# Folding three of eight q k products on VectorE before the head sums on TensorE, with q and k chunked by every second feature

## The chip, the cores and the metric

The kernel runs on one core of a Trainium2 chip. The metric is the device time of one execution in microseconds (us); of several runs the median is taken. Engines are called by their names in the profile: PE is TensorE's matmul, PEld its weight load, DVE is VectorE, ACT ScalarE, POOL GpSimd, SP the engine that issues most DMAs.

## What is computed

One input x of 2048 tokens by 512 features goes through a layer norm to xn. Two branches read xn and both are added to x.

```python
def _A_ref(x, wqkv, wo):             # H = 32 heads of Dh = 16
    W, dil = (8, 2)
    q, k, v = ...                    # from x @ wqkv
    off = jnp.arange(W) * dil        # each token sees itself and 7 tokens before it, in steps of 2
    logits = jnp.einsum('bhsd,bhswd->bhsw', q, kg) * scale
    attn = _softmax(where(mask, logits, -1e9))
    return einsum('bhsw,bhswd->bhsd', attn, vg) ... @ wo

def _B_ref(x, w_in, w_sp, b_sp, w_out):
    z = _gelu(x @ w_in)              # 2 x 688 features
    z1, z2 = z[..., :688], _layernorm(z[..., 688:])
    g = jnp.einsum('ts,bsf->btf', w_sp, z2) + b_sp
    return (z1 * g) @ w_out

out = x + _A_ref(xn, wqkv, wo) + _B_ref(xn, w_in, w_sp, b_sp, w_out)
```

## The kernel before

The order of instructions on every engine is the order in which the program writes them; nothing is reordered by a planner. Tiles wait for one another through semaphores, and a tile that lies over memory of a closed pool waits for the last use of what lay there. Tokens are handled in 16 tiles of 128. For attention they are split into two halves, hb = 0 and 1, of 1024 tokens, and each half into four groups of 256.

*Layer norm, transposes, z2.* In the first 30 us of the span the layer norm is made and xn is transposed into xnT (feature on the partition). z2_tile(i) (L235) makes one tile of gelu(xn @ w_in) for the second half of the features.

*q and k.* qk_pair (L289) and qk_chunk (L277) multiply 512 tokens with a chunk c of 128 columns of wqkv, 4 chunks for q and 4 for k, four accumulating matmuls of 512 columns each. ScalarE copies the result into qk[hb], with one feature per partition. Chunk c holds features 128c to 128c + 127, which is eight whole heads.

*Logits.* The eight distances are handled in pairs. products(hb, p) (L318) multiplies q with k at two distances, all four chunks, in one VectorE instruction of 8192 elements a partition. reduce_heads(hb, p) (L327) sums over the 16 features of a head, which lie on partitions: a 0/1 matrix rsel sends the 128 partitions of chunk c to its heads, and the four chunks accumulate in PSUM. The four token groups go to four 32-column tiles of the array, which run side by side. ScalarE copies the sums into lg (L329). softmax_top (L334 to L339), softmax_exp (L342, on ScalarE) and softmax_norm (L348 to L353) make the weights a_sb.

*Values.* v_pair (L302) makes v with a strided view of wv: every 16th column, for one feature of all 32 heads.

*The gated branch.* z2_norm (L269) normalises the 16 tiles of z2 on VectorE, one instruction each. mix(j) (L512) is the product of row block j of w_sp with all z2, 32 matmuls; ScalarE empties it into gs (L515), and the next row block j + 5 is loaded by a transposing DMA on SP. z1_tile(j) (L524) makes the matching tile of z1 with a gelu on ScalarE (L529), and gate_out(j) (L534) multiplies the two on VectorE; SP sends the product transposed into uT. There are three z1 tiles and four gs tiles.

mix and z1_tile take pairs of PSUM banks in turn. For tiles above 3 there are two pairs, so that mix(j + 1) takes the pair that mix(j) had, and z1_tile(j + 1) that of z1_tile(j).

*Between the stages.* From mix(0) on, TensorE goes through mix and z1_tile for j = 0 to 15. In the first three of these VectorE still ends the logits and the softmax; then from a queue of steps, av_ops, vector_work(us) takes steps until their written costs add up to the argument. A step is one product of v with the weights (L578, pw), an add (L583, L585, L587 into op), or softmax_norm for hb = 1. The order at this place is:

```python
g0 = mix(0)
products(1, 3)
z1_tile(0, g0)
g1 = mix(1)
softmax_norm(0, lgp)
z1_tile(1, g1)
gate_out(0)
g2 = mix(2)
reduce_heads(1, 2)
reduce_heads(1, 3)
softmax_top(1)
gate_out(1)
z1_tile(2, g2)
softmax_exp(1)
```

*The end.* out_b (L659) multiplies uT with w_out and out_a (L668) multiplies op with wo. For token groups jj = 0 and 1 out_b comes first, for jj = 2 and 3 out_a. op_rest carries two of the 16 features of op into free rows of uT, for hb = 0 by SP and for hb = 1 by ScalarE's queue. store adds x (the xr tiles) on VectorE (L675) and sends the result out; sums for jj = 2 take the banks that the stores of jj = 0 empty.

Of the kernel before, what the change touches and what calls it, by code (L numbers as in the profile page):

```python
# [7 lines left out]
BF16 = mybir.dt.bfloat16  # L8
F32 = mybir.dt.float32
ACT = mybir.ActivationFunctionType  # L10
ALU = mybir.AluOpType
PSUM = bass.MemoryType.PSUM

P = 128
# [3 lines left out]
C = D // P  # L18
# [11 lines left out]
TG = SB // NG  # L30
# [17 lines left out]
def kernel(  # L48
# [16 lines left out]
    V = nc.vector  # L65
    A = nc.scalar
    G = nc.gpsimd
    PE = nc.tensor
# [7 lines left out]
    const = ctx.enter_context(tc.tile_pool(name="const", bufs=1))  # L76
    base = ctx.enter_context(tc.tile_pool(name="base", bufs=1))
# [4 lines left out]
    pair_b = ExitStack()  # L82
# [4 lines left out]
    def bank_pair(name, two=False):  # L87
        turn[0] += 1
        pool = ps_b if turn[0] % 3 == 0 and not two else ps_a
        return pool.tile([P, 2, 512], F32, name=name, tag="mm")  # L90
# [9 lines left out]
    def spin(n):  # L100
        for _ in range(n):
# [5 lines left out]
    G.memset(ident[:], 0.0)  # L107
    G.affine_select(out=ident[:], in_=ident[:], compare_op=ALU.not_equal, fill=1.0,
                    base=0, pattern=[[-1, P]], channel_multiplier=1)
    rsel = const.tile([P, C, 32], BF16, name="rsel")  # L110
    G.memset(rsel[:], 1.0)
    for c in range(C):
        G.affine_select(out=rsel[:, c, :], in_=rsel[:, c, :], compare_op=ALU.is_ge, fill=0.0,
                        base=128 * c, pattern=[[-16, 32]], channel_multiplier=1)
        G.affine_select(out=rsel[:, c, :], in_=rsel[:, c, :], compare_op=ALU.is_ge, fill=0.0,
                        base=15 - 128 * c, pattern=[[16, 32]], channel_multiplier=-1)
    mask = const.tile([32, W, HALO], F32, name="mask")
    G.memset(mask[:], 0.0)
    G.affine_select(out=mask[:], in_=mask[:], compare_op=ALU.is_ge, fill=NEG,
                    base=-DIL * (W - 1), pattern=[[DIL, W], [1, HALO]], channel_multiplier=0)  # L120
# [22 lines left out]
    xnT = rpool.tile([P, C, S], BF16, name="xnT")  # L143
# [11 lines left out]
    wqk = e1.tile([P, C, 2, D], BF16, name="wqk")  # L155
# [95 lines left out]
    def z2_moments(i):  # L251
        for hh in range(2):
            V.bn_stats(zst[:, i, hh, :], z2[:, i, hh * FHALF:(hh + 1) * FHALF])
        V.bn_aggr(zmv[:, i, :], zst[:, i, :, :])
# [11 lines left out]
    def z2_norm():  # L266
        V.reciprocal(zrstd[:], zrstd[:])
        for i in range(NT):
            V.tensor_scalar(z2[:, i, :], z2[:, i, :], zmv[:, i, 0:1], zrstd[:, i:i + 1],  # L269
                            ALU.subtract, ALU.mult)  # L270

    def qk_chunk(b, c):
        tsl = slice(b * 512, (b + 1) * 512)
        pq = bank_pair("pq")
        for s in range(2):
            for kc in range(C):
                PE.matmul(pq[:, s, :], wqk[:, kc, s, c * P:(c + 1) * P], xnT[:, kc, tsl],  # L277
                          start=(kc == 0), stop=(kc == C - 1))
        at = HALO + b % 2 * 512
        A.copy(qk[b // 2][:, :, c, at:at + 512], pq[:])  # L280

    def qk_pair(b, s, c2):

        tsl = slice(b * 512, (b + 1) * 512)
        pq = bank_pair("pq")
        for cc in range(2):
            c = 2 * c2 + cc
            for kc in range(C):
                PE.matmul(pq[:, cc, :], wqk[:, kc, s, c * P:(c + 1) * P], xnT[:, kc, tsl],  # L289
                          start=(kc == 0), stop=(kc == C - 1))  # L290
        at = HALO + b % 2 * 512
        A.copy(qk[b // 2][:, s, 2 * c2:2 * c2 + 2, at:at + 512], pq[:])
# [15 lines left out]
    def shifted(ap):  # L308

        return bass.AP(ap.tensor, ap.offset, [ap.ap[0], [DIL, 2]] + list(ap.ap[1:]))  # L310

    lg = [lgp.tile([P, W, TG], BF16, name="lg") for _ in range(NB)]
    prs = {}

    def products(hb, p):
        pr = (prx if (4 * hb + p) % 3 == 2 else prp).tile([P, 2, C, SB], BF16, name="pr")
        off = HALO - DIL * (W - 1 - 2 * p)
        V.tensor_tensor(pr[:], qk[hb][:, 0, :, HALO:HALO + SB].unsqueeze(1).broadcast_to([P, 2, C, SB]),  # L318
                        shifted(qk[hb][:, 1, :, off:off + SB]), ALU.mult)
        prs[hb, p] = pr  # L320

    def reduce_heads(hb, p):
        pr = prs.pop((hb, p))
        pl = ps_aux.tile([P, 2, TG], F32, name="pl", tag="aux")
        for c in range(C):
            for k in range(NG):
                PE.matmul(pl[32 * k:32 * k + 32, :, :], rsel[:, c, :], pr[:, :, c, k * TG:(k + 1) * TG],  # L327
                          start=(c == 0), stop=(c == C - 1), tile_position=(0, 32 * k))
        A.activation(lg[hb][:, 2 * p:2 * p + 2, :], pl[:], ACT.Copy, scale=float(DH) ** -0.5)  # L329

    def softmax_top(hb):
# [9 lines left out]
    def softmax_exp(hb):  # L341
        A.activation(a_sb[:, :, hb * TG:(hb + 1) * TG], lg[hb][:], ACT.Exp)  # L342

    def softmax_norm(hb, pool):
        hsl = slice(hb * TG, (hb + 1) * TG)
        s4 = pool.tile([P, 4, TG], F32, name="s4", bufs=1)
        r1 = pool.tile([P, TG], BF16, name="r1", bufs=1)
        V.tensor_tensor(s4[:], a_sb[:, 0:4, hsl], a_sb[:, 4:8, hsl], ALU.add)  # L348
        V.tensor_tensor(s4[:, 0:2, :], s4[:, 0:2, :], s4[:, 2:4, :], ALU.add)
        V.tensor_tensor(s4[:, 0, :], s4[:, 0, :], s4[:, 1, :], ALU.add)  # L350
        V.reciprocal(s4[:, 0, :], s4[:, 0, :])
        V.tensor_copy(r1[:], s4[:, 0, :])
        V.tensor_tensor(a_sb[:, :, hsl], a_sb[:, :, hsl],  # L353
                        r1[:].unsqueeze(1).broadcast_to([P, W, TG]), ALU.mult)
# [3 lines left out]
    def load_wsp(j):  # L358
        t = wspp.tile([P, NT, P], BF16, name="wspT")
        SP.dma_start_transpose(t[:], B_w_sp[j * P:(j + 1) * P, :])  # L360
        wsps[j] = t
# [97 lines left out]
    reduce_heads(0, 1)  # L459
    reduce_heads(0, 2)  # L460
    products(0, 3)
    z2_moments(7)
    z2_moments(8)
    v_pair(0)
# [26 lines left out]
    v_pair(5)  # L491
    reduce_heads(1, 1)
    products(1, 2)
    softmax_exp(0)
    v_pair(6)
    v_pair(7)
# [11 lines left out]
    def mix(j):  # L508
        pg = bank_pair("pg", j > 3)
        for k in range(NT):  # L510
            for hh in range(2):
                PE.matmul(pg[:, hh, 0:FHALF], wsps[j][:, k, :], z2[:, k, hh * FHALF:(hh + 1) * FHALF],  # L512
                          start=(k == 0), stop=(k == NT - 1))
        gs = gsp.tile([P, 2, FHALF], BF16, name="gs")
        A.activation(gs[:], pg[:, :, 0:FHALF], ACT.Identity, bias=b_col[:, j:j + 1])  # L515
        if j + 5 < NT:
            load_wsp(j + 5)
        return gs

    def z1_tile(j, gs):  # L520
        pz = bank_pair("pz1", j > 3)
        for hh in range(2):
            for kc in range(C):
                PE.matmul(pz[:, hh, 0:FHALF], xnT[:, kc, j * P:(j + 1) * P],  # L524
                          w_z1[:, kc, hh * FHALF:(hh + 1) * FHALF],
                          start=(kc == 0), stop=(kc == C - 1))
        z1 = z1p.tile([P, FPAD], BF16, name="z1")
        G.memset(z1[:, FH:FPAD], 0.0)  # L528
        A.activation(z1[:, 0:FH].rearrange("p (a b) -> p a b", a=2), pz[:, :, 0:FHALF], ACT.Gelu_apprx_tanh)  # L529
        gate[j] = (gs, z1)  # L530

    def gate_out(j):
        gs, z1 = gate.pop(j)
        V.tensor_tensor(z1[:, 0:FH], gs[:].rearrange("p a b -> p (a b)"), z1[:, 0:FH], ALU.mult)  # L534
        SP.dma_start_transpose(uT[:, :, j * P:(j + 1) * P], z1[:])

    g0 = mix(0)
    products(1, 3)
    z1_tile(0, g0)
    g1 = mix(1)  # L540
    softmax_norm(0, lgp)
    z1_tile(1, g1)
    gate_out(0)
    g2 = mix(2)
    reduce_heads(1, 2)
    reduce_heads(1, 3)
    softmax_top(1)
    gate_out(1)
    z1_tile(2, g2)
    softmax_exp(1)  # L550
    att.close()

# [42 lines left out]
    def vector_work(us):  # L595
        while us > 0:
            t = next(work, None)
            if t is None:
                return
            us -= t  # L600
# [6 lines left out]
        SP.dma_start(xr[:], x_g[jj // 2, jj % 2])  # L607
        xrs.append(xr)

    vector_work(2.0)  # L610
    for j in range(3, NT):
        z1_tile(j, mix(j))
        if j == 3:
            pair_b.close()
            ps_o = [ctx.enter_context(tc.tile_pool(name="ps_o0", bufs=4, space=PSUM, reuse_waits="tile"))]
        vector_work(4.6)
        gate_out(j - 1)
        if j == 5:
            SP.dma_start(wout[:, 0:MCH - 1, :], B_w_out[0:(MCH - 1) * P, :].rearrange("(m p) n -> p m n", p=P))
            SP.dma_start(wout[0:FTAIL, MCH - 1, :], B_w_out[(MCH - 1) * P:FH, :])  # L620
            for e in range(2):
                SP.dma_start(wout[64 + 32 * e:96 + 32 * e, MCH - 1, :],
                             A_wo.rearrange("(h d) n -> d h n", d=DH)[DHA + e])
        if 6 <= j < 10:
            k = j - 6
            SP.dma_start(wo_r[32 * k:32 * k + 32, :, :], A_wo.rearrange("(h d) n -> h d n", d=DH)[:, 0:DHA, :])
        if 11 <= j < 13:
            load_xr(j - 11)
        if j == 13:
            op_rest(0, SP)  # L630
# [95 lines left out]
```

## Time and profile before

| what | value |
|---|---|
| median of 3 runs | 205.79 us (205.72 to 206.36) |
| profiled execution | 206.46 us |
| its span in the profile | 204.6 us |
| granted TensorE clock | 0.998 |
| matmuls | 1660 |
| q and k: L277 and L289 | 128 matmuls, 128x512 |
| head sums: L327 | 128 matmuls, 128x512, 32 columns of the array each |
| products: L318 | 8 of 4.42 us on VectorE |

The span is the time that the profile covers; the 1.9 us around it belong to the execution. A row of the groups gives the line of the program, the engine, the operation with its output and inputs and their shapes, how many there were, the busy time in us and the mean of one in ns, and the engine's idle time before them with what ended it. Busy times of one engine may overlap, above all those of matmuls, whose ends are modelled; the time that a series of matmuls takes is read from the chain or the timeline.

### The profile page before, as it was taken

The page shows a single profiled execution, that of the slowest core. Times are in us where ns is not written, and L with a number is a line of the kernel's source. Part 1 is how long each engine was busy: PE and PEld are TensorE (multiplying, and loading weights), DVE is VectorE, ACT ScalarE, POOL GpSimd, SP SyncE. Part 2 cuts the span into 40 slices and gives each one's busy share as a digit, 9 for nine tenths or more (in the row PEclk, how much of TensorE's full clock was granted, in tenths as well). Part 3 has the DMA queues.
Part 4 walks back from the last instruction along what each step waited for, and adds up shares of the span by engine and source line. Part 5 has one row for each costly group of instructions (what it writes and reads, how often), then busy time and mean ns, then how long its engine had stood idle before and what let it go on. Part 6 is the DMA issues. An engine that isn't in the chain of part 4 may idle for free.

```text
span 204.6 us, 4053 instructions
## 1 busy us (share of the span) xinstructions
PE 200.0 (98%) x1660; PEld 120.8 (59%) x1660; DVE 171.3 (84%) x210; ACT 89.4 (44%) x130; POOL 16.7 (8%) x82
## 2 busy tenths in 40 slices
PE   7899999999999999999999999999999999999994
PEld 7655554546666666656666666666666664444442
DVE  4799949979699999959999999999999988335163
ACT  4768986665889875335733321223333311000000
POOL 5035640000000100100000000000000000000000
PEclk9999999999999999999999999999999999999999
DMA  5984857996000006435957799999656224015633
GB/s 175 323 259 79 177 108 151 217 198 143 0 0 3 3 0 98 91 75 126 125 112 160 181 196 194 219 175 178 130 144 141 54 48 80 10 37 161 235 106 99
DMA packets 67410, 25.63 MB, mean 125 GB/s; under 512 B 57168, under 2 KB 67264, under 8 KB 67264
## 3 DMA queue, kind: packets, MB, share of 16 engines
q1 hardware_dynamic: 66976, 25.24, 56.7%
q8 instruction: 13, 0.21, 0.5%
q10 hardware_dynamic: 416, 0.14, 0.3%
q14 instruction: 5, 0.04, 0.1%
HBM read 9.79 MB, written 2.10 MB: 58 GB/s over the span
## 4 chain that ended last, share of the span: by engine, by line
PE 95%; DMA 3%; SPq 1%; DVE 0%; issue 0%
PE pg L512 37%; PE pq L277 10%; PE po L659 10%; PE pz L524 9%; PE pzb L235 9%; PE pv L302 7%; PE po L668 6%; PE pl L327 3%; PE pq L289 3%; DMA w_z<-in_B_w_in_dram 3%; PE po L641 1%; SPq L178 0%; PE pt L218 0%; SPq L176 0%; DVE ot L643 0%; SPq L175 0%
## 5 line engine op out<-in xcount | busy, mean ns | idle before, releaser
L512 PE MATMUL pg<-z,wspT 128*128 128x344 bf16 x512 | 77.3, 310 | 0.0
L512 PEld LDWEIGHTS <-wspT 128*128 128x128 bf16 x512 | 50.0, 98 | 24.9 <-issue 0.4
L318 DVE TENSOR_TENSOR pr<-qk 128x8192 bf16<-128x8192 bf16 x8 | 35.0, 4420 | 2.7 <-ACT qk L280 1.5
L515 ACT ACTIVATE gs<-pg,b_col 128x688 bf16<-128x688 f32 x16 | 13.3, 832 | 54.4 <-PE pg L512 54.4
L578 DVE TENSOR_TENSOR pw<-vp,a_sb 128x4096 bf16<-128x4096 bf16 x16 | 36.1, 2284 | 0.0
L277 PE MATMUL pq<-xnT,wqk 128*128 128x512 bf16 x96 | 21.4, 380 | 0.0
L524 PE MATMUL pz<-w_z,xnT 128*128 128x344 bf16 x128 | 21.3, 310 | 0.0
L235 PE MATMUL pzb<-w_z,xnT 128*128 128x344 bf16 x128 | 20.0, 310 | 0.5 <-DMA w_z<-in_B_w_in_dram 0.3
L659 PE MATMUL po<-wout,uT 128*128 128x512 bf16 x90 | 19.8, 380 | 0.0
L583 DVE TENSOR_TENSOR pw<-pw 128x4096 bf16<-128x4096 bf16 x8 | 18.3, 2288 | 0.1
L675 DVE TENSOR_TENSOR ot<-po,xr 128x512 bf16<-128x512 f32 x15 | 9.7, 686 | 9.3 <-PE po L668 6.9
L235 PEld LDWEIGHTS <-xnT 128*128 128x128 bf16 x128 | 12.3, 98 | 7.3 <-issue 0.5
L524 PEld LDWEIGHTS <-xnT 128*128 128x128 bf16 x128 | 12.4, 98 | 6.5 <-issue 0.4
L277 PEld LDWEIGHTS <-wqk 128*128 128x128 bf16 x96 | 9.3, 98 | 11.1 <-issue 0.4
L280 ACT CAST qk<-pq 128x1024 bf16<-128x1024 f32 x12 | 12.1, 1012 | 6.8 <-PE pq L277 6.8
L659 PEld LDWEIGHTS <-uT 128*128 128x128 bf16 x90 | 8.7, 98 | 10.7 <-issue 0.4
L302 PE MATMUL pv<-xnT,wv 128*32 128x512 bf16 x256 | 14.8, 380 | 0.0
L529 ACT ACTIVATE z<-pz 128x688 bf16<-128x688 f32 x16 | 11.9, 743 | 5.6 <-PE pz L524 5.2
L242 ACT ACTIVATE z<-pzb 128x688 bf16<-128x688 f32 x16 | 11.8, 739 | 2.2 <-PE pzb L235 2.2
L528 POOL MEMSET z<- 128x80 bf16 x16 | 3.1, 199 | 115.9 <-DMA uT<-z 61.2
L302 PEld LDWEIGHTS <-wv 128*32 128x32 bf16 x256 | 9.8, 140 | 4.2 <-issue 0.3
L668 PE MATMUL po<-wo_r,op 32*128 32x512 bf16 x224 | 12.3, 375 | 0.0
(85 smaller groups left out, 178.7 us busy)
## 6 DMA issues: line engine op xcount, KB each, us to landing
xr<-in_A_x_dram SPq DMA_DIRECT2D x4, 512.0 KB, 4.2
out_dram<-ot SPq DMA_DIRECT2D x15, 128.0 KB, 1.8
wo_r<-in_A_wo_dram SPq DMA_DIRECT2D x4, 448.0 KB, 4.9
xq<-in_A_x_dram SPq DMA_DIRECT2D x2, 512.0 KB, 7.8
wqk<-in_A_wqkv_dram SPq DMA_DIRECT2D x2, 512.0 KB, 7.8
w_z<-in_B_w_in_dram SPq DMA_DIRECT2D x2, 344.0 KB, 4.4
w_z<-in_B_w_in_dram SPq DMA_DIRECT2D x1, 688.0 KB, 5.7
wout<-in_B_w_out_dram SPq DMA_DIRECT2D x1, 640.0 KB, 4.6
```

The source lines that it names most:

```text
L235: PE.matmul(pz[:, hh, 0:FHALF], xnT[:, kc, i * P:(i + 1) * P], w_z2[:, kc, hh * FHALF:(hh + 1) * FHALF], start=(kc == 0), stop=(kc == C - 1))
L277: PE.matmul(pq[:, s, :], wqk[:, kc, s, c * P:(c + 1) * P], xnT[:, kc, tsl], start=(kc == 0), stop=(kc == C - 1))
L280: A.copy(qk[b // 2][:, :, c, at:at + 512], pq[:])
L302: PE.matmul(pv[32 * k:32 * k + 32, dd, :].rearrange("p (b t) -> p b t", b=NB), wv_v[:, kc, 2 * d2 + dd, :], xnT_g[:, kc, :, k, :], start=( ...
L318: V.tensor_tensor(pr[:], qk[hb][:, 0, :, HALO:HALO + SB].unsqueeze(1).broadcast_to([P, 2, C, SB]), shifted(qk[hb][:, 1, :, off:off + SB]), ...
L512: PE.matmul(pg[:, hh, 0:FHALF], wsps[j][:, k, :], z2[:, k, hh * FHALF:(hh + 1) * FHALF], start=(k == 0), stop=(k == NT - 1))
L515: A.activation(gs[:], pg[:, :, 0:FHALF], ACT.Identity, bias=b_col[:, j:j + 1])
L524: PE.matmul(pz[:, hh, 0:FHALF], xnT[:, kc, j * P:(j + 1) * P], w_z1[:, kc, hh * FHALF:(hh + 1) * FHALF], start=(kc == 0), stop=(kc == C - 1))
L578: V.tensor_tensor(pw[:], shifted(vp[:, :, hb, off:off + P]), a_sb[:, 2 * p:2 * p + 2, osl].unsqueeze(2).broadcast_to([P, 2, DH, P]), ALU.mult)
L583: V.tensor_tensor(pws[p - 1][:], pws[p - 1][:], pw[:], ALU.add)
L659: PE.matmul(pos[jj, k][:], uT[:, m, i * P:(i + 1) * P], wout[:, m, :], start=first and m == 0, stop=not first and m == MCH - 1)
L668: PE.matmul(pos[jj, k][:], op[32 * k:32 * k + 32, d, jj * P:(jj + 1) * P], wo_r[32 * k:32 * k + 32, d, :], start=first and d == 0, stop=(n ...
```

## The change

The features of q and k are put into chunks in another way. Chunk c now holds the features 256 (c mod 2) + 2j + (c div 2) for j = 0 to 127: every second feature of one half of the 512. Chunks c and c + 2 then hold, on the same partition, two neighbouring features of the same head. So one matrix rsel serves both, with 8 partitions to a head, and has two parts in place of four.

Because of that the two can be added before the sum over partitions. A new function fold does it on VectorE, in place, for three of the eight product tiles, (0, 3), (1, 2) and (1, 3); for these reduce_heads runs over two chunks instead of four. The weights of q and k are read with a step of two elements.

Around mix(0) to mix(3) the order is changed: gate_out(0) goes ahead of softmax_norm(0), gate_out(1) and z1_tile(2) ahead of reduce_heads(1, 2), and mix(3) and z1_tile(3) ahead of softmax_exp(1). The step of av_ops that came ahead of mix(3) is no longer taken there (vector_work(2.0) is gone), so that each later call takes steps that come one earlier in the queue than before.

```diff
-    rsel = const.tile([P, C, 32], BF16, name="rsel")
+    rsel = const.tile([P, 2, 32], BF16, name="rsel")
     G.memset(rsel[:], 1.0)
-    for c in range(C):
-        G.affine_select(out=rsel[:, c, :], in_=rsel[:, c, :], compare_op=ALU.is_ge, fill=0.0,
-                        base=128 * c, pattern=[[-16, 32]], channel_multiplier=1)
-        G.affine_select(out=rsel[:, c, :], in_=rsel[:, c, :], compare_op=ALU.is_ge, fill=0.0,
-                        base=15 - 128 * c, pattern=[[16, 32]], channel_multiplier=-1)
+    for g in range(2):
+        G.affine_select(out=rsel[:, g, :], in_=rsel[:, g, :], compare_op=ALU.is_ge, fill=0.0,
+                        base=128 * g, pattern=[[-8, 32]], channel_multiplier=1)
+        G.affine_select(out=rsel[:, g, :], in_=rsel[:, g, :], compare_op=ALU.is_ge, fill=0.0,
+                        base=7 - 128 * g, pattern=[[8, 32]], channel_multiplier=-1)
...
+    wqk_v = wqk[:].rearrange("p k s (g j e) -> p k s e g j", g=2, e=2)
+
     def qk_chunk(b, c):
...
-                PE.matmul(pq[:, s, :], wqk[:, kc, s, c * P:(c + 1) * P], xnT[:, kc, tsl],
+                PE.matmul(pq[:, s, :], wqk_v[:, kc, s, c // 2, c % 2], xnT[:, kc, tsl],
...
     def qk_pair(b, s, c2):
...
-                PE.matmul(pq[:, cc, :], wqk[:, kc, s, c * P:(c + 1) * P], xnT[:, kc, tsl],
+                PE.matmul(pq[:, cc, :], wqk_v[:, kc, s, c // 2, c % 2], xnT[:, kc, tsl],
...
+    def fold(hb, p):
+
+        pr = prs[hb, p]
+        V.tensor_tensor(pr[:, :, 0:2, :], pr[:, :, 0:2, :], pr[:, :, 2:4, :], ALU.add)
+        folded.add((hb, p))
+
+    folded = set()
+
     def reduce_heads(hb, p):
         pr = prs.pop((hb, p))
         pl = ps_aux.tile([P, 2, TG], F32, name="pl", tag="aux")
-        for c in range(C):
+        n = 2 if (hb, p) in folded else C
+        for c in range(n):
             for k in range(NG):
-                PE.matmul(pl[32 * k:32 * k + 32, :, :], rsel[:, c, :], pr[:, :, c, k * TG:(k + 1) * TG],
-                          start=(c == 0), stop=(c == C - 1), tile_position=(0, 32 * k))
+                PE.matmul(pl[32 * k:32 * k + 32, :, :], rsel[:, c % 2, :], pr[:, :, c, k * TG:(k + 1) * TG],
+                          start=(c == 0), stop=(c == n - 1), tile_position=(0, 32 * k))
...
     products(0, 3)
+    fold(0, 3)
     z2_moments(7)
...
     products(1, 2)
+    fold(1, 2)
     softmax_exp(0)
...
     g0 = mix(0)
     products(1, 3)
+    fold(1, 3)
     z1_tile(0, g0)
     g1 = mix(1)
+    gate_out(0)
     softmax_norm(0, lgp)
     z1_tile(1, g1)
-    gate_out(0)
     g2 = mix(2)
+    gate_out(1)
+    z1_tile(2, g2)
     reduce_heads(1, 2)
     reduce_heads(1, 3)
     softmax_top(1)
-    gate_out(1)
-    z1_tile(2, g2)
+    z1_tile(3, mix(3))
     softmax_exp(1)
     att.close()
...
-    vector_work(2.0)
+    pair_b.close()
+    ps_o = [ctx.enter_context(tc.tile_pool(name="ps_o0", bufs=4, space=PSUM, reuse_waits="tile"))]
     for j in range(3, NT):
-        z1_tile(j, mix(j))
-        if j == 3:
-            pair_b.close()
-            ps_o = [ctx.enter_context(tc.tile_pool(name="ps_o0", bufs=4, space=PSUM, reuse_waits="tile"))]
+        if j > 3:
+            z1_tile(j, mix(j))
         vector_work(4.6)
         gate_out(j - 1)
```

## The prediction

> **What bounds the kernel now.** I read four views: the page's busy shares with the shares of the chain, the chain in order of time, the groups with shapes kept apart, and the timelines of VectorE and ScalarE. First the busy shares and the chain's shares.
>
> ```profile
> PE 200.0 (98%) x1660; PEld 120.8 (59%) x1660; DVE 171.3 (84%) x210; ACT 89.4 (44%) x130; POOL 16.7 (8%) x82
> ...
> PE 95%; DMA 3%; SPq 1%; DVE 0%; issue 0%
> ```
>
> TensorE is busy for 98% of the span and makes 95% of the chain; VectorE makes none of it. So a matmul taken out anywhere after the first 8 us shortens the end by its own time, provided nothing else becomes late. The chain in order of time (start, length, what) prices the matmuls in question and gives the moments that TensorE will need data:
>
> ```profile
> 43.99 2.72 PE pl L327 x48
> ...
> 63.78 0.86 PE pl L327 x16
> ...
> 73.28 4.77 PE pg L512 x32
> ...
> 89.72 1.84 PE pl L327 x32
> ```
>
> A call of reduce_heads is 16 matmuls in 0.86 us, 54 ns each, since four run side by side in 32-column tiles: the 380 ns in its row below is one matmul's latency. The groups (instruction, shape, count | busy, mean ns | idle):
>
> ```profile
> L583 DVE TENSOR_TENSOR pw<-pw 128x4096 bf16<-128x4096 bf16 x8 | 18.3, 2288 | 0.1
> ...
> L302 PEld LDWEIGHTS <-wv 128*32 128x32 bf16 x256 | 9.8, 140 | 4.2 <-issue 0.3
> ...
> L327 PE MATMUL pl<-pr,rsel 128*32 128x512 bf16 x128 | 7.8, 380 | 0.0
> ...
> L277 PEld LDWEIGHTS <-wqk 128*128 128x128 bf16 x96 | 9.3, 98 | 11.1 <-issue 0.4
> ...
> L327 PEld LDWEIGHTS <-rsel 128*32 128x32 bf16 x128 | 3.3, 97 | 3.6 <-issue 0.7
> ```
>
> L583 is an add of exactly a fold's size. The three load rows are for the strided weights, below. Last, where VectorE has room (start, length, what, idle before):
>
> ```profile
> 53.08 8.76 DVE L318 TENSOR_TENSOR pr<-qk 128x8192 bf16<-128x8192 bf16 x2 [1.50 <-ACT qk L280]
> ...
> 69.17 6.00 DVE L269 TENSOR_SCALAR z<-z,zmv,zrstd 128x688 bf16<-128x688 bf16 x16
> 75.09 8.75 DVE L318 TENSOR_TENSOR pr<-qk 128x8192 bf16<-128x8192 bf16 x2
> ...
> 92.24 0.69 DVE L336 TENSOR_TENSOR m<-lg 128x1024 bf16<-128x1024 bf16 x1 [2.27 <-ACT lg L329]
> ...
> 95.32 4.49 DVE L578 TENSOR_TENSOR pw<-vp,a_sb 128x4096 bf16<-128x4096 bf16 x2
> ...
> 169.52 0.52 DVE L534 TENSOR_TENSOR z<-gs,z 128x688 bf16<-128x688 bf16 x1 [1.35 <-ACT z L529]
> ```
>
> It idles 1.50 us at 51.6, 2.27 at 90, 1.35 at 168, and is without work from 175.83 to 182.18.
>
> **TensorE, what is removed.** Each of three folded products needs 8 matmuls in place of 16: 0.43 us less, together 1.30. Of this 0.43 is gained before mix(0), the rest before mix(3). Putting reduce_heads(1, 2) and (1, 3) behind z1_tile(2) changes the order, not the amount.
>
> **TensorE, strided weights.** The 128 matmuls of q and k (216 ns each in the chain: 6.91 us for 32) now load every second column of wqk. No row has that stride. Contiguous loads take 98 ns, and 97 for 32 columns. The wv load, every 16th element, takes 140 for 32 columns, 43 more, or 1.3 ns a column. The lower bound is 98, no change: the load reads no less than before, so a gain is excluded. The upper bound is 1.3 x 128 on top, 98 + 172 = 270 ns, 54 over the matmul that hides it: 128 x 54 ns = 6.9 us. Between them stands what pv does with its strided loads: 64 matmuls in 3.45 us, so four loads, 128 strided columns, fit into every 216 ns with no loss. A step of 2 is nearer to 1 than to 16; I take about 100 to 150 ns, hidden under 216, cost 0. [...]
>
> **VectorE, what is added.** A fold is 2.29 us by L583; start to start it is 2.21, and its product before it loses 0.13 of overlap (4.43 and a gap in place of 4.34). So 2.34 each, 7.0 in all. I follow the delay through the queue:
> - fold(0, 3) fills the 1.50 idle before products(1, 0), whose copy of q and k is there at 53.05 as before: delay 0.84. z2_norm ends at 76.0, was 75.17. mix(0) reads its 16 tiles one per 0.29 us and comes 0.43 earlier, at 72.85: the last is wanted at 77.23. Margin 1.2 us.
> - fold(1, 2) and fold(1, 3): products(1, 2) starts at 75.9, fold(1, 3) ends near 89.4. TensorE runs mix(2) to 89.3, z1_tile(2) to 90.5, reduce_heads(1, 2) to 90.9, and only then wants fold(1, 3). Margin 1.5. In the old order reduce_heads(1, 3) would come 1.2 earlier; that is what its move is worth.
> - Then gate_out(0), softmax_norm(0) (5.69) and gate_out(1) in one run to 95.9. softmax_top(1) has its logits by 92.5, so the 2.27 us wait is gone too, and ends at 98.6 (94.9 before, with gate_out(1) still to come). The first pw starts at 98.5 instead of 95.32: 3.2 us late, which is 7.0 less 1.50 and 2.27.
>
> **ScalarE, the tightest place.** Its timeline before:
>
> ```profile
> 96.35 1.91 ACT L342 ACTIVATE a_sb<-lg 128x2048 bf16<-128x2048 bf16 x1
> 98.16 0.82 ACT L515 ACTIVATE gs<-pg,b_col 128x688 bf16<-128x688 f32 x1
> ```
>
> softmax_exp(1), with a table load of 1.28 ahead, waits for softmax_top(1). Behind it stands the emptying of a mix. In the new order it is issued after mix(3) and z1_tile(3), so that only gs of mix(4) is behind it. It runs from 98.65 to 101.85; mix(4) ends at 103.33 - 1.30 = 102.03. mix(5) takes the same pair of banks after z1_tile(4) (1.17), and gs needs 0.83, so 0.3 more may be lost: margin 0.5 us. A table load for gelu then follows, 4 us before z1_tile(5) wants its banks.
>
> **The queue to the end.** vector_work(2.0) is gone, so each gate_out has one pw fewer ahead (2.26): the gates come about 0.9 us later than before, and TensorE is 1.3 earlier. A walk through the same costs puts gate_out(5) at 119.0, gate_out(9) at 141.1, gate_out(14) at 167.1. In the trace a z1 tile is free some 4.8 us after the gate_out three before it, and gelu of tile 8 then starts at 126.6, against 123.8: margin 2.8, the smallest. The wait of 1.35 at 168 shrinks to about 0.7. VectorE ends its av work at 179.0 instead of 175.83. Who waits for that: the stores of jj = 0, whose sums are ready at 180.8 (margin 1.8; out_a(2) wants their banks); op_rest(1, A), eight DMAs that ScalarE issues in 5.05 us and that land 1.8 later, at 185.9, and out_b(2, 0) wants them at 189.9 (margin 4.0); and out_a(3), at 186.9. Nothing is late.
>
> **At no cost.** On SP the order of issues stays as it was (row blocks 5 and 6, gate 0, block 7, gate 1, block 8). GpSimd has four selects of 0.2 us less at 1.6 to 3.4 us and sits idle till 12.7; its wout memset goes behind the z1 memset of tile 3 (92.96 in the trace), and wout is loaded at 113.7.
>
> **Sum.** The profiled execution took 206.46 for a span of 204.6. The span becomes 203.3, that execution 205.2. It was 0.67 above the median of the runs, 205.79; from the median I forecast 204.5.
>
> **Rivals.**
> - *Strided loads bind.* Place: the 12 to 52 us stretch, where 128 matmuls stand back to back. It decides once a load exceeds 216 ns. [...] Against: pv loses nothing with a wider step, and 118 ns of cover. Price at the upper bound 6.9: 211.4, slower. At 230 ns it takes 1.8 and the time is 206.3. Chance 0.09.
> - *VectorE's or ScalarE's delay reaches TensorE.* The 0.5 us ahead of mix(5) decides, then the 1.2 and 1.5. For it: VectorE is over 95% busy from 60 to 90 us, so no slip is made up. Against: each margin is counted from rows with the same shapes. A slip of 0.8 to 1.8 us costs 0.3 to 1.3: 204.8 to 205.8. Chance 0.12.
> - *A fold runs at half the rate,* since it reads two separate blocks: 4.5 us. products read such blocks too, at 0.54 ns an element, so it is unlikely. z2_norm's end at 78.2 would stall mix(0) by 1.0 and fold(1, 3) at 96 would stall reduce_heads(1, 3) by 4: 204.5 + 5.0 = 209.5, slower. Chance 0.03.
>
> **How the numbers follow.** The forecast has 0.76, with 204.0 to 205.0 as its own range: the runs before differ by 0.6, and the 0.1 that 32 matmuls at 89.72 take beyond twice 0.86 may go. With the second rival the range reaches 205.8; what lies beyond is the 0.12 of the others. About 0.3%, 0.6 us, is what a measurement of this kernel can tell from no change; faster by that is below 205.2. It has the forecast and a third of the second rival, 0.80; within it, 0.08; slower, 0.12.
>
> **What would show it.** L327 with 104 matmuls, 0.43 us for each folded product; the q and k chain still 6.91 us per 32 and its loads below 216 ns; three adds of 2.29; first pw near 98.5; av work done near 179; mix(5) behind z1_tile(4) with no gap. Wrong would be: q and k spread out, or a TensorE gap ahead of mix(0), reduce_heads(1, 3), mix(5) or out_a(2).

## The result and the profile after

The changed kernel takes 205.19 us, the kernel before 206.11 (medians of 20 runs each). The ratio is 0.9956, 95% interval 0.9943 to 0.997: faster by 0.9 us. The forecast was faster by 1.30, a ratio of 0.9937, which this interval does not hold: the sign and the mechanism came out and the size is short. Of the 0.7 us between the forecast time of 204.5 and 205.19, 0.3 lies in the starting value: three runs had put the kernel before at 205.79, twenty put it at 206.11. The profiled execution took 205.51 with a span of 203.5, 1.1 below that of before.

First the page's busy shares and the shares of the chain of the changed kernel:

```profile
PE 198.0 (97%) x1629; PEld 120.2 (59%) x1636; DVE 177.9 (87%) x213; ACT 89.3 (44%) x130; POOL 15.4 (8%) x78
...
PE 92%; DMA 4%; SPq 2%; issue 1%; DVE 0%
```

TensorE is 2.0 us less busy; VectorE has 6.6 us more and still no part of the chain. 24 weight loads are gone (1636 against 1660); of the matmuls seven more records are missing, which is part of the 2.0. DMA has 4% of the chain where it had 3%, and it is another load: of w_z2 before, of wqk now.

The groups of the changed kernel (busy, mean ns | idle before), the add, the head sums and the strided loads:

```profile
L328 DVE TENSOR_TENSOR pr<-pr 128x4096 bf16<-128x4096 bf16 x3 | 6.9, 2292 | 0.1
L339 PE MATMUL pl<-pr,rsel 128*32 128x512 bf16 x104 | 6.5, 380 | 0.0
...
L280 PEld LDWEIGHTS <-wqk 128*128 128x128 bf16 x96 | 9.3, 98 | 11.0 <-issue 0.4
```

The folds cost what L583 said, 2.29, and the load with a step of two takes the 98 ns of the contiguous one. The chain in order of time shows where TensorE gained, and at its start where it lost:

```profile
4.28 8.18 DMA wqk<-in_A_wqkv_dram
12.46 0.27 issue
12.73 6.64 PE pq L292 x30
19.37 3.50 PE pzb L236 x24
...
63.99 0.43 PE pl L339 x8
...
90.66 0.98 PE pl L339 x16
```

A folded product takes 0.43, two together 0.98 where it was 1.84. But the first block of q and k now hangs on the load of its weights, and TensorE's timeline has a gap after one matmul:

```profile
12.02 0.38 PE L292 MATMUL pq<-xnT,wqk 128*128 128x512 bf16 x1
12.73 6.64 PE L292 MATMUL pq<-xnT,wqk 128*128 128x512 bf16 x30 [0.33 <-DMA wqk<-in_A_wqkv_dram]
19.21 3.66 PE L236 MATMUL pzb<-w_z,xnT 128*128 128x344 bf16 x24
```

Before, the same 32 matmuls ran through:

```profile
12.10 7.07 PE L289 MATMUL pq<-xnT,wqk 128*128 128x512 bf16 x32
19.00 3.66 PE L235 MATMUL pzb<-w_z,xnT 128*128 128x344 bf16 x24
```

One record of the 32 is missing after the change, so the block is better measured from its start to the z2 matmuls behind it: 7.19 in place of 6.90, which is 0.29 lost.

This cuts the span into two parts that can be compared. The first q and k block is followed by 24 matmuls of z2; their start in the chain was 19.16 before and is 19.37 after:

```profile
12.26 6.91 PE pq L289 x32
19.16 3.50 PE pzb L235 x24
```

From there to the end it was 204.6 - 19.16 = 185.4 and is 203.5 - 19.37 = 184.1: 1.3 less, the forecast. The head of the kernel, up to that point, lost 0.2 in these two profiles: 0.29 by the gap, less 0.08 because q started earlier.

Last, VectorE's and ScalarE's timelines at the places that were thought tight:

```profile
70.06 6.00 DVE L270 TENSOR_SCALAR z<-z,zmv,zrstd 128x688 bf16<-128x688 bf16 x16
...
87.08 2.29 DVE L328 TENSOR_TENSOR pr<-pr 128x4096 bf16<-128x4096 bf16 x1
...
98.49 4.49 DVE L594 TENSOR_TENSOR pw<-vp,a_sb 128x4096 bf16<-128x4096 bf16 x2
...
181.10 2.48 DVE L690 TENSOR_TENSOR ot<-po,xr 128x512 bf16<-128x512 f32 x4 [1.82 <-PE po L683]
```

```profile
98.65 1.28 ACT L354 ACT_TABLE_LOAD   x1 [0.24 <-DVE lg L351]
99.95 1.91 ACT L354 ACTIVATE a_sb<-lg 128x2048 bf16<-128x2048 bf16 x1
102.28 0.83 ACT L529 ACTIVATE gs<-pg,b_col 128x688 bf16<-128x688 f32 x1 [0.43 <-PE pg L526]
```

z2_norm ends at 76.06, fold(1, 3) at 89.37, the first pw starts at 98.49, the exponential ends 0.43 ahead of the gs behind it, and VectorE waits 1.82 for the sums of jj = 0. No wait of TensorE on VectorE or ScalarE appears behind the first block.

### The profile page after: what moved, and what is told of

Read it like the earlier page. It is cut to its first block, busy times and chain, and to the rows that moved or that the text cites. A ratio compares the mean times of both kernels' runs of the same rounds, so it can differ in the third digit from the quotient of the medians.

```text
span 203.5 us, 3996 instructions
## 1 busy us (share of the span) xinstructions
PE 198.0 (97%) x1629; PEld 120.2 (59%) x1636; DVE 177.9 (87%) x213; ACT 89.3 (44%) x130; POOL 15.4 (8%) x78
## 4 chain that ended last, share of the span: by engine, by line
PE 92%; DMA 4%; SPq 2%; issue 1%; DVE 0%
PE pg L526 37%; PE pq L280 10%; PE po L674 9%; PE pz L538 9%; PE pzb L236 7%; PE pv L305 7%; PE po L683 6%; DMA wqk<-in_A_wqkv_dram 4%; PE pq L292 3%; PE pl L339 3%; PE po L656 1%; SPq L179 0%; SPq L183 0%; SPq L171 0%; SPq L177 0%
## 5 line engine op out<-in xcount | busy, mean ns | idle before, releaser
L529 ACT ACTIVATE gs<-pg,b_col 128x688 bf16<-128x688 f32 x16 | 13.3, 833 | 55.2 <-PE pg L526 55.2
L674 PE MATMUL po<-wout,uT 128*128 128x512 bf16 x88 | 19.3, 379 | 0.2 <-issue 0.2
L542 POOL MEMSET z<- 128x80 bf16 x16 | 2.6, 164 | 127.7 <-DMA uT<-z 76.1
```

The lines of the kernel that those rows point to most:

```text
L674: PE.matmul(pos[jj, k][:], uT[:, m, i * P:(i + 1) * P], wout[:, m, :], start=first and m == 0, stop=not first and m == MCH - 1)
```

## The experiments

The theory: the gain is the 24 matmuls and nothing else; the shift of VectorE's work is kept from TensorE by the new order; and what is missing is a new wait of q's weights. Rivals: the order brings part of the gain; the order is not needed; the wait was a chance of one execution.

**The changed kernel once more.** No edit.

> The changed kernel once more, as the measure for the three run beside it. If the wait ahead of the second q matmul is part of the change, TensorE stands idle between the first and the second matmul of q and k again, until the load of k's weights has landed (near 12.5 us); if that wait was a chance of one execution, the gap is gone. Time 0.9 us below the kernel before, some 205.2.

205.36 us, ratio to the kernel before 0.9946 (0.9924 to 0.9968). The gap is there again and larger:

```profile
11.41 0.38 PE L292 MATMUL pq<-xnT,wqk 128*128 128x512 bf16 x1
12.71 6.64 PE L292 MATMUL pq<-xnT,wqk 128*128 128x512 bf16 x30 [0.93 <-DMA wqk<-in_A_wqkv_dram]
```

One matmul runs as soon as z2 lets it, at 11.41; the second stands until the second wqk load, that of k, has landed at 12.44 (issued at 4.28, 8.16 in the chain). The kernel before has no such wait: there q ran on from 12.10, though k's load landed only at 12.6 (issued at 4.3, 8.3 to landing).

**Separate tiles for the weights of q and k.**

```diff
-    wqk = e1.tile([P, C, 2, D], BF16, name="wqk")
+    wqk = [e1.tile([P, C, D], BF16, name=n) for n in ("wq", "wk")]
...
-        SP.dma_start(wqk[:, :, s, :], wqkv_r[:, :, s * D:(s + 1) * D])
+        SP.dma_start(wqk[s][:], wqkv_r[:, :, s * D:(s + 1) * D])
...
-    wqk_v = wqk[:].rearrange("p k s (g j e) -> p k s e g j", g=2, e=2)
+    wqk_v = [w[:].rearrange("p k (g j e) -> p k e g j", g=2, e=2) for w in wqk]
...
-                PE.matmul(pq[:, s, :], wqk_v[:, kc, s, c // 2, c % 2], xnT[:, kc, tsl],
+                PE.matmul(pq[:, s, :], wqk_v[s][:, kc, c // 2, c % 2], xnT[:, kc, tsl],
...
```

> The changed kernel with the weights of q and of k in two tiles, so that no matmul of q can be tied to the load of k. Theory (the strided view ties q's second matmul to k's load): no gap at 12 us, q and k start 0.2 to 0.4 us earlier than in the changed kernel, span 203.2 or 203.3 and the full 1.30 below the kernel before. Rival (the DMA was late by chance, or q waits for its own load): no difference from the changed kernel.

204.92 us, ratio 0.9934 (0.9911 to 0.9956), span 202.6. The gap is gone:

```profile
11.45 3.62 PE L292 MATMUL pq<-xnT,wq 128*128 128x512 bf16 x15
14.90 3.62 PE L292 MATMUL pq<-xnT,wk 128*128 128x512 bf16 x16
18.36 3.66 PE L236 MATMUL pzb<-w_z,xnT 128*128 128x344 bf16 x24
```

That k's load can land after q has begun without a wait is seen in the kernel with every fourth feature below, which has the same split: q began at 12.81, and k's load, issued at 4.3, landed 9.0 later, at 13.3. So the wait belongs to the strided view over a tile that two loads write: not to the strided read, which is without a wait in both, and not to the shared tile, which the kernel before has as well. How the wait follows from such a view is not shown. In the chain the 24 z2 matmuls start at 18.52, and 184.1 follow, as in the changed kernel. A second series gave 205.09 and 0.9943 (0.9922 to 0.9963), with the 24 matmuls at 19.03 in its profile:

> split_weights once more, as the measure for the fourth fold with cover beside it: 204.9, and from the end of the first q and k block (32 matmuls) to the end of the span 184.1 us, as in the changed kernel.

The stretch behind them is again 184.1. The head of this second profile is longer for causes that come before q and k: 0.6 of idle ahead of a transpose and 0.2 for w_z2.

**No folds.** The changed kernel without its three calls of fold.

```diff
-    fold(0, 3)
...
-    fold(1, 2)
...
-    fold(1, 3)
```

> The changed kernel without its three folds: strided weights and new order stay, 128 matmuls for the head sums. Theory (the gain is the 24 matmuls): 1.30 above the changed kernel, so 0.2 to 0.4 slower than the kernel before. Rival (the gain comes from the new order, the folds are neutral): as fast as the changed kernel, 0.9 below the kernel before.

206.23 us, ratio 0.9995 (0.9974 to 1.0016), 0.9 above the changed kernel beside it. In the chain the 24 matmuls start at 18.67 of 204.1: 185.4 follow, 1.3 more than with the folds:

```profile
18.67 3.50 PE pzb L236 x24
```

Here the wait for k's weights was only 0.23, since they landed earlier: the weight load that waited for them began at 11.80, against 12.50 in the changed kernel. The expected 1.30 over the changed kernel came out as 0.9 in the medians, and the expected 0.2 to 0.4 over the kernel before is not seen.

**The new order alone.** The kernel before, with contiguous weights and no fold, in the order of the changed kernel.

> The kernel before with the new order around mix(0) to mix(3) alone: contiguous weights, no folds. Theory: TensorE has the same work and no wait in either order, so the time of the kernel before within 0.1. Rival (the order brings part of the gain): 0.3 or more below it. Against no_fold it also shows the strided weights by themselves: 0.2 to 0.4 by the theory of the wait.

206.1 us, ratio 0.9998 (0.9972 to 1.0024). In the chain the 24 matmuls start at 18.69 of 204.1, so 185.4 follow again: the order brings nothing by itself.

```profile
18.69 3.50 PE pzb L235 x24
```

**The folds in the old order.** The changed kernel with the lines between mix(0) and the loop as they were.

> The changed kernel with its folds and strided weights, in the order of the kernel before. Theory: fold(1, 3) still ends before reduce_heads(1, 3) would stall for more than 0.3 us, softmax_top(1) ends near 98.1, the exponential stands ahead of gs of mix(3) and runs to 101.4, gelu of tile 3 ends at 104.2 and TensorE waits 2.0 us for it ahead of z1_tile(4): 207.3 against 205.3 for the changed kernel. Rival (the order is no matter): 205.3. Second rival (the wait for fold(1, 3) is the larger one): a gap ahead of reduce_heads(1, 3).

208.01 us, ratio 1.009 (1.0056 to 1.0125): slower than the kernel before. The expected 207.3 is met by the profiled execution, 207.22; the median is 0.8 higher, and the clocks given under the next experiment bear on that. TensorE's timeline has the gap where it was expected and as long, 2.01 for 2.0:

```profile
97.04 4.83 PE L526 MATMUL pg<-z,wspT 128*128 128x344 bf16 x32
103.88 1.33 PE L538 MATMUL pz<-w_z,xnT 128*128 128x344 bf16 x8 [2.01 <-ACT z L543]
```

There is no gap ahead of reduce_heads(1, 3), so the second rival falls.

**softmax_exp(1) put back, alone.**

```diff
-    z1_tile(3, mix(3))
     softmax_exp(1)
+    z1_tile(3, mix(3))
```

> The kernel with split weights, and softmax_exp(1) put back ahead of mix(3) and z1_tile(3) in ScalarE's queue; all else as it was. Theory (the place of this one instruction is what keeps VectorE's delay off TensorE): softmax_top(1) ends at 97.7 as before, the exponential runs to 101.0, and gs of mix(3), ready at 95.6, gelu's table load and gelu of tile 3 queue up behind it till 103.9. z1_tile(4) wants that pair of banks at 101.4, so TensorE stands for 2.5 us and the time is 207.4, slower than the kernel before. Rival (the delay is covered by spare banks in either order): 204.9, as split_weights.

208.67 us, the median of four runs, ratio 1.0107 (1.0058 to 1.0155); the profiled execution took 207.41. The gap is 2.44 for 2.5:

```profile
96.92 4.83 PE L526 MATMUL pg<-z,wspT 128*128 128x344 bf16 x32
104.19 1.33 PE L538 MATMUL pz<-w_z,xnT 128*128 128x344 bf16 x8 [2.44 <-ACT z L543]
```

ScalarE's timeline of this run shows what queued behind the exponential:

```profile
99.45 1.91 ACT L354 ACTIVATE a_sb<-lg 128x2048 bf16<-128x2048 bf16 x1
101.27 0.81 ACT L529 ACTIVATE gs<-pg,b_col 128x688 bf16<-128x688 f32 x1
102.10 1.28 ACT L543 ACT_TABLE_LOAD   x1
103.39 0.74 ACT L543 ACTIVATE z<-pz 128x688 bf16<-128x688 f32 x1
```

With all other moves in place, that of one ScalarE instruction makes the difference between a gain of 1.3 and a loss of 1.3 behind the first block (in the timelines the 24 matmuls start at 18.72 of 205.6 here and at 19.00 of 204.6 before). The other moves were not tried one by one.

The median lies 1.3 above what the gap explains, and the granted TensorE clock of the single runs goes with it. Two of the four had a clock of 0.998 or more and took 207.41 and 208.0; the other two had 0.99 and spans of 207.6 and 208.2, as 205.6 / 0.99 = 207.7 would have it (an estimate). Three of the eight runs of the old order had 0.992 and spans of 207.0 to 207.9. No other run of this case with its clock on record was below 0.998. Only the two kernels with a gap of 2 us had such runs; why is not shown.

**A fourth fold.** split_weights with fold(0, 0) behind products(0, 0).

> split_weights with a fourth fold, of (0, 0), right behind its product. Theory (each fold is worth 0.43 us as long as VectorE has room, and the room is used up): VectorE idles 1.18 us ahead of products(0, 3), so half of the fold's 2.34 is covered; products(0, 2) ends 2.3 later, near 45.5, and reduce_heads(0, 2) wants it at 44.7: a gap of 0.7, more than the 0.43 gained. z2_norm comes 1.2 later, its margin ahead of mix(0) is about used up. Time 204.9 to 205.4, not faster than split_weights. Rival (a fold is a gain anywhere, since TensorE is the bound): 204.5.

205.69 us, ratio 0.9968 (0.9948 to 0.9988): not faster than split_weights. The gap is 0.82 for 0.7, and the stretch behind the first block is 203.5 - 18.88 = 184.6, 0.5 more than with three folds (0.82 less 0.43 makes 0.4):

```profile
45.94 1.05 PE L339 MATMUL pl<-pr,rsel 128*32 128x512 bf16 x16 [0.82 <-DVE pr L321]
```

**The fourth fold with cover.**

```diff
     reduce_heads(0, 0)
+    v_pair(0)
     reduce_heads(0, 1)
+    v_pair(1)
     reduce_heads(0, 2)
...
-    v_pair(0)
-    v_pair(1)
...
     z1_tile(3, mix(3))
+    z1_tile(4, mix(4))
     softmax_exp(1)
...
-        if j > 3:
+        if j > 4:
             z1_tile(j, mix(j))
```

> fourth_fold, with TensorE's order changed so that what the fold delays is asked for later: v_pair(0) between reduce_heads(0, 0) and (0, 1), v_pair(1) between (0, 1) and (0, 2), and mix(4) and z1_tile(4) also ahead of softmax_exp(1). Theory (a fold is worth 0.43 where its 2.34 us on VectorE are covered): the 0.8 us gap ahead of reduce_heads(0, 2) is gone, z2_norm ends just in time for mix(0), and the stretch from the end of the first q and k block is 183.6 to 183.8, 0.3 to 0.4 less than split_weights: 204.5. Rival (VectorE has no room for a fourth fold anywhere): a new gap ahead of mix(0), reduce_heads(1, 3) or out_a(2) takes it back, 184.1 or more.

204.77 us, ratio 0.9933 (0.9909 to 0.9957); span 202.5. The gap of 0.82 is gone and the stretch behind the first block is 202.5 - 18.60 = 183.9, 0.2 less than with three folds, where 0.43 was to be had. In the chain mix(0) takes the rest back, 5.02 for the 4.77 of the other kernels, since z2_norm now ends at 76.34:

```profile
71.83 5.02 PE pg L527 x32
```

This is the lowest median of the series, below both kernels; against split_weights the intervals overlap.

**Every fourth feature.** split_weights with chunks 4j + c, and 4 partitions to a head in rsel.

```diff
-    wqk_v = [w[:].rearrange("p k (g j e) -> p k e g j", g=2, e=2) for w in wqk]
+    wqk_v = [w[:].rearrange("p k (j e) -> p k e j", e=4) for w in wqk]
...
-                PE.matmul(pq[:, s, :], wqk_v[s][:, kc, c // 2, c % 2], xnT[:, kc, tsl],
+                PE.matmul(pq[:, s, :], wqk_v[s][:, kc, c], xnT[:, kc, tsl],
...
```

> split_weights with chunks of every fourth feature, so that the q and k loads read every fourth column. The load took 98 ns with step 1 and with step 2. By the wv row (139 ns for 32 columns with step 16), if the excess grows with the step: some 110 to 140 ns, hidden. [...] In both cases q and k keep 216 ns a matmul and the span is that of split_weights, 202.6.

The load takes 114 ns, within the 110 to 140 that the wv row gave; the q and k chain keeps 6.64 for 30 matmuls:

```profile
L280 PEld LDWEIGHTS <-wq 128*128 128x128 bf16 x48 | 5.4, 114 | 4.7 <-issue 0.4
...
13.25 6.64 PE pq L292 x30
```

The span of this single run (206.04 us) is 204.0, not the expected 202.6, but 1.36 of the 1.4 over split_weights lies ahead of q: w_z2 landed at 8.83 and z2 stood 1.24 for it. Behind the first block 184.1 follow.

**Contiguous loads for v.**

```diff
-                              wv_v[:, kc, 2 * d2 + dd, :], xnT_g[:, kc, :, k, :],
+                              wv[:, kc, 32 * (2 * d2 + dd):32 * (2 * d2 + dd) + 32], xnT_g[:, kc, :, k, :],
```

> split_weights with contiguous columns in place of every 16th for the weights of v; its v has other features than the reference's. It measures the step by itself. Theory (the step of 16 makes the load longer, and the cover hides it): the wv load falls from 139 ns to 97, that of rsel, and v_pair keeps 1.73 us for 32 matmuls. Rival (the 139 ns have another cause): 139 stay. If strided loads cost TensorE time, v_pair gets shorter.

The load falls from 139 to 97 ns, so the step is the cause, and v_pair keeps 1.73 us for 32 matmuls: the longer load costs TensorE nothing.

```profile
L305 PEld LDWEIGHTS <-wv 128*32 128x32 bf16 x256 | 7.0, 97 | 6.8 <-issue 0.3
...
64.89 1.73 PE pv L305 x32
```

The changed kernel, with its step of 16, has:

```profile
L305 PEld LDWEIGHTS <-wv 128*32 128x32 bf16 x256 | 9.6, 139 | 4.4 <-issue 0.3
...
64.42 1.73 PE pv L305 x32
```

This single run took 205.82 us with a span of 204.0; its 24 z2 matmuls start late, at 19.89, and 184.1 follow as with the step.

## Why the prediction was right, and where it was short

- *TensorE, what is removed.* Right: 0.43 a fold, and 1.3 behind the first block, shown three ways: changed against before (184.1 and 185.4), no_fold (185.4), reorder_only (185.4). All six profiles with three folds in the new order and softmax_exp(1) in its new place have 184.1.
- *VectorE.* Right to a few tenths: z2_norm's end 76.0 forecast and 76.06 found, fold(1, 3) 89.4 and 89.37, first pw 98.5 and 98.49, end of the av work 179.0 and 179.28, margin of the stores 1.8 and 1.82. The wait ahead of gate_out(15) did not shrink to 0.7: it is 1.51, because the walk with mean costs ran 0.7 late by gate_out(14).
- *ScalarE, the tightest place.* Right: the exponential was to end at 101.85 and gs to be ready at 102.03; they came at 101.86 and 102.28. old_order and exp_back show that this order is what the gain hangs on.
- *Strided weights.* The load was right (98 within 98 to 270, hidden), and the rival of binding loads falls: step 2 took the 98 ns of the contiguous load and step 4 took 114, its longest 133, and with both the chain kept 6.64 us for 30 matmuls. The limit of 216 ns in that rival and its chance of 0.09 were the author's estimates; no run shows a load that long, so the limit was not tested.
- *The term that failed* is the cost 0 of the strided weights, and it failed outside the load: the view made q's second weight load wait for the DMA of k's weights (the tie, below). The profiles show it as 0.33, 0.93, 0.23 and 0.5 us of TensorE's idle time in the four kernels that have the view over one tile (changed, again, no_fold, old_order); measured from q's start to the z2 matmuls, the block of the first three took 0.29, 0.88 and 0.18 more than the 6.90 of before. The kernels with split tiles have none of it. The trace of before could have shown the risk: there k's load landed at 12.6, half a microsecond after q began.
- *Luck.* 205.19 lies outside the forecast's own range of 204.0 to 205.0. The range reached to 205.8 for another reason, a delay of VectorE or ScalarE that reaches TensorE, and that did not happen. That the time came out inside it is owed to this width.

In the two profiles the tie accounts for what is missing (1.1 of 1.3). How much it makes of the missing 0.4 in the medians is not settled. The head of the kernel varies by itself: the 24 matmuls started between 18.52 and 19.89 in profiles without the tie, up to 1.2 us of that by the landing of w_z2; and a late w_z2 hides part of the tie (0.6 us of wait for it and a gap of 0.33 in the first profile, no wait and 0.93 in the second). The ratios with split tiles, 0.9934 and 0.9943, stand beside 0.9946 and 0.9956 of the changed kernel, the right way, but with overlapping intervals; the forecast 0.9937 lies inside those of split_weights.

## What to carry to other kernels

Where one engine has no gaps, work taken off it pays its full time (here 1.3 us for three folds of 0.43), as long as each wait that the extra work delays elsewhere is followed to the instruction queued behind it; here a single exponential in a strict queue decided between 1.3 us gained and 1.3 lost. Cover is a sum that can be used up: three folds of 2.34 us fitted, a fourth paid half after its consumers had been moved back. When a view of a tile is changed, look at what the reads are now made to wait for, not only at how long they take.

## What the runs showed of the hardware

A weight load of q and k, 128 columns, took 98 ns at steps of 1 and 2 elements and 114 at 4; one of v, 32 columns, took 97 contiguous and 139 at a step of 16. All of it was hidden under matmuls of 512 columns: q and k kept 6.64 us for 30 matmuls at steps 1, 2 and 4, v_pair 1.73 for 32 at steps 1 and 16. The execution's time varied with the landing of the loads in the first 13 us: TensorE waited between 0 and 1.24 us for w_z2, and in single profiles the q and k block began between 11.4 and 12.8. The granted TensorE clock was 0.990 to 0.992 in five of the twelve runs of the two kernels with a gap of 2.0 to 2.4 us on TensorE, and 0.998 or more in every other run that has it on record.
